# Attention and two MoE stages on one core: a tile's scores in one run of PSUM columns, and what moves with it

## The chip, the core and the metric

One NeuronCore of a Trainium2 chip runs the whole program. The metric is the device time of one execution in microseconds (us): median 1417.6 over three runs, 1417.41 to 1417.85. Five engines work side by side and meet through semaphores: TensorE (PE in the profile: matrix products and transposes, results in PSUM), VectorE (DVE), ScalarE (ACT), GpSimd (POOL) and SyncE (SP, which issues most DMAs). PSUM has eight banks of 512 float32 columns in each of 128 partitions.

## The reference

```python
# attention: B=8, H=8, S=576, D=64; keys and values averaged over 8 neighbours: 72 of each
k_p = k.reshape(B, H, 72, 8, D).mean(axis=3); v_p = ...            # the same
scores = scale * q @ k_p.T;  scores -= max(scores)
attn = exp(scores) / (sum(exp(scores)) + 1e-9);  x = attn @ v_p    # -> 4608 x 512
# moe1: each token goes to its best of 8 experts (512 -> 1024 -> 512)
e = argmax(x @ w_gate + modality_bias[modality_id])
x = gate * (relu(x @ w1[e]) @ w2[e])
# moe2, dense: 512 -> 2048 -> 512
h = x @ w_in;  out = (h * clip(h + 3, 0, 6) / 6) @ w_out
```

## The kernel before

**Attention (0 to about 199 us).** 36 tiles of 128 query rows; one tile holds all eight heads and its 8 x 72 = 576 scores. The fifth tile of a batch holds the last 64 rows of two batches. The loop over tiles is software-pipelined and written out in order: iteration i transposes the exponentials e of tile i (`stage_t`, five transposes and ScalarE's copy eT), takes the exponentials of tile i+2 (`stage_e`, two on ScalarE), scales the second half of the output of tile i-1 (`stage_x`, four on ScalarE), transposes q of tile i+4 (`stage_q`, ScalarE's copy qT), makes the scores of tile i+3 (`stage_s`: eight matmuls, then on VectorE the maximum, L287, and the subtraction, L290 or L293, each once for four heads), and multiplies tile i with the values (`stage_a`: twelve matmuls ups, two halves; on VectorE the sums rs, a reciprocal and the scaling of the first half). Since each engine works in the order in which its instructions were issued, this order is the schedule.

Each batch also needs its keys and values: `pool_kv` averages them (VectorE, L175), `prep` transposes four heads at a time (kvps) and copies them into the block-diagonal key matrix bd (one half by VectorE, L213, one by ScalarE, L214) and vT (L218); `prep2` multiplies the values with the gate weights (pw, L228, L230), which VectorE puts into vb. `sched1` and `sched2` say at which tile. `put_p` makes bp, the form of bd for the mixed tiles. After every group of tiles (`GROUPS`) the routing of its tokens is worked out: `route` and `route_b` give a list `fill` of small operations, of which `run_fill` issues one at fixed places of the stages, mostly on VectorE; `route_b` first issues six short matmuls rps (L416), a running count of tokens per expert.

PSUM in the attention: three banks ps_s, taken in turn by scores (one bank for four heads), kvps, pw and rps; two for the transposes of e; two for ups; one, ps_q, for the transposes of q.

**moe1 (to about 650 us).** Units of 400 tokens of one expert: unit 0, then units in a hardware loop, then two `fs` units and a last one. A unit walks over eight blocks f of the hidden layer: twelve matmuls ph, ScalarE's relu hi and VectorE's rest lo (values are split in two parts for precision), and twelve matmuls y of the block before, over four output banks. In the last block the next unit's tokens are transposed (pt, L856): chunks 0 and 1 ahead of y of block 6, chunks 2 and 3 ahead of y of block 7. Each chunk becomes xhi (ScalarE) and xlo (VectorE) before its bank of two is free again; tkr is a small copy after chunk 0. At the unit's end four copies bring y to SBUF (L1024). Beside this the units prepare moe2's weights: w_in by `conv` (18 operations a call, `ops`), blocks of w_out by `wo_conv`, those in `EARLY` within the `fs` units, those in `REST` in moe2.

**moe2 (to the end).** 6 x 8 `quad`s of products with split weights. Conversions of w_out (`cops`, nine operations a block, on VectorE and ScalarE) are dealt out over the quads of the first of six token groups: two at each of seven places.

Of the kernel before, what the change touches and what calls it, by code (L numbers as in the profile page):

```python
# [19 lines left out]
P = 128  # L20
# [21 lines left out]
EARLY = (0, 8, 1, 9, 2, 10)  # L42
REST = (3, 11, 4, 12, 5, 13, 6, 14, 7, 15)
# [30 lines left out]
def attention(tc, g, moe, ins, xr_d):  # L74
# [122 lines left out]
    def put_v(b, ps):  # L197
        vTs[b] = p2.tile([P, HK], F32, name="vT", tag="vT")
        nc.scalar.copy(vTs[b][64:128].rearrange("p (z x) -> p z x", z=2), ps.rearrange("p (z x) -> p z x", z=2)[64:128, :, 0:288])

    def prep_v(b):
        ps = kv_ps()
        kv_t(b, 2 * D, ps)
        put_v(b, ps)

    def prep(b, z, which="kv"):
        ps = ps_s.tile([P, 512], F32, name="kvps", tag="s")
# [14 lines left out]
    def prep2(b):  # L222
        vT = vTs.pop(b)
        x = kvq.pop(b)
        pw = ps_s.tile([P, 512], F32, name="pw", tag="s")
# [22 lines left out]
    def stage_q(i):  # L248
        b, t = tiles[i]
        ps = ps_q.tile([P, 512], F32, name="qps", tag="q")  # L250
# [16 lines left out]
    def stage_s(i):  # L267
# [11 lines left out]
        mx = p3.tile([P, 2, 4, 1], F32, name="mx", tag="mx")  # L279
        for x in range(2):  # L280
            ps = ps_s.tile([P, 512], F32, name="sps", tag="s")
            for a in range(2 * x, 2 * x + 2):
                for b, p0, p1 in halves(i):
                    rhs = bd[b % 3][:, 4 * hh + a] if t < 4 else bp[b % 3][:, a]
                    nc.tensor.matmul(ps[p0:p1, 144 * (a % 2):144 * (a % 2) + 144], o[:, a, p0:p1], rhs, start=True, stop=True)
            s4 = ps[:, 0:288].rearrange("p (h k) -> p h k", k=SP)
            nc.vector.tensor_reduce(mx[:, x], s4, AX.X, ALU.max)  # L287
            run_fill()
            if t < 4:
                nc.vector.tensor_tensor(d.rearrange("p t (h k) -> p h t k", k=SP)[:, 2 * x:2 * x + 2], s4.rearrange("p (h t) k -> p h t k", t=2),  # L290
                                        mx[:, x].rearrange("p (h t) o -> p h t o", t=2).to_broadcast([P, 2, 2, SP]), op=ALU.subtract)
            else:
                nc.vector.tensor_tensor(d[:, x].rearrange("p (h k) -> p h k", k=SP), s4, mx[:, x].to_broadcast([P, 4, SP]), op=ALU.subtract)  # L293
            run_fill()
# [28 lines left out]
    def stage_a(i):  # L323
        o = ETt.pop(i)
        if i == NTI - 2:
            u = [ps_s.tile([P, 512], F32, name="ups", tag="s")[:, 0:4 * UX].rearrange("p (j x) -> p j x", x=UX) for z in range(2)]
        else:
            u = [ps_u.tile([P, 4, UX], F32, name="ups", tag=f"u{z}") for z in range(2)]
# [80 lines left out]
    def route_b(new=lambda: ps_s.tile([P, 512], F32, name="rps", tag="s")):  # L409
# [77 lines left out]
    sched1, sched2 = {}, {}  # L487
# [10 lines left out]
    wps = ps_q.tile([P, 512], F32, name="wps", tag="q")  # L498
    for _ in range(WU):
        nc.tensor.matmul(wps, zb[:, 0:P], zb[:, 0:512], start=True, stop=True)  # L500
# [24 lines left out]
    kv_t(0, D, ps, (1,))  # L525
    put_k(0, ps, (1,))
# [7 lines left out]
    prep_v(0)  # L534
# [6 lines left out]
    at2(0, lambda: pool_kv(1, 1, v_, rs=(4,)))  # L541
# [7 lines left out]
    at2(3, lambda: prep2(1))  # L549
    for b in range(2, B):  # L550
# [9 lines left out]
        at2(first[b] - o + 2, lambda b=b: (put_p(b), prep2(b)))  # L560
# [17 lines left out]
    for i in range(NTI - 3):  # L578
# [24 lines left out]
        for fn_ in sched1.get(i, ()):  # L603
            fn_()
# [18 lines left out]
    xq = lambda: ps_q.tile([P, 512], F32, name="xps", tag="q")  # L623
    xs = lambda: ps_s.tile([P, 512], F32, name="xps", tag="s")
# [174 lines left out]
def moe1(tc, g, xr_d, tok_d, y_d, s_d, w1, w2, w_in):  # L799
# [83 lines left out]
    def store_y(col):  # L883
# [440 lines left out]
```

## Time and profile before

| | |
|---|---|
| median of three runs | 1417.6 us (1417.41 to 1417.85) |
| the profiled execution | 1416.87 us, its span 1415.1 us |
| mean granted TensorE clock | 0.992 |
| TensorE busy | 1368.4 us, 97% of the span, 7594 instructions |
| VectorE busy | 947.2 us, 67%, 1929 |
| ScalarE busy | 627.6 us, 44%, 1276 |
| GpSimd busy | 159.3 us, 11%, 191 |

A busy share is a mean over three stages with different limits, so stretches are read apart. A timeline row gives start, length, engine, line of the kernel, operation, what it writes and reads with its shape, and in brackets how long the engine was idle before it and whose end released it. A row may stand for several equal instructions (xN). Matmul ends are modelled: a row's length may overlap the next row. A row on a stretch gives its two ends and its length, then busy us and instructions of TensorE, of its weight loads, of VectorE, ScalarE and GpSimd, the granted TensorE clock as a share of full speed, the DMA share and GB/s. A row on a group gives line, engine, operation, its shape and count, busy us and the mean ns of one, and the idle time before them by releaser.

### The profile page before, as it was taken

To read this page: it belongs to the slowest core of one execution; us is meant where nothing else is said; L and a number is where in the kernel's file an instruction comes from. 1 tells how busy PE (TensorE), PEld (TensorE's weight loads), DVE (VectorE), ACT (ScalarE), POOL (GpSimd) and SP (SyncE) were. 2 spreads that over 40 slices of the span, in tenths; PEclk is the share of its full clock that TensorE was granted. 3 is DMA by queue.
4 is the path that set the end of the run, shared out by engine and by line. 5 is a ranking of instruction groups with operands and counts; after the bars stand their busy time and mean duration, and the time that the engine had idled before them with its cause. 6 is when DMAs were issued, how large, how long until landed. Compare 5 with 4: busy or idle time off the path is not lost.

```text
span 1415.1 us, 24118 instructions
## 1 busy us (share of the span) xinstructions
PE 1368.4 (97%) x7594; PEld 1263.5 (89%) x7594; DVE 947.2 (67%) x1929; ACT 627.6 (44%) x1276; POOL 159.3 (11%) x191
## 2 busy tenths in 40 slices
PE   7998989999999999999999999999999999999997
PEld 5888878999999999998888889888988888888886
DVE  6999785788888887876777445645644564465443
ACT  3576664555555554553444333423432343243322
POOL 3132331111111111100000100100010010001001
PEclk8899999999999999999999999999999999999999
DMA  9996356777777776675653544554354455345441
GB/s 254 314 273 203 108 167 197 245 245 246 246 244 243 243 241 199 188 223 169 202 163 114 184 142 120 159 162 119 120 181 140 120 150 173 116 119 164 115 116 67
DMA packets 229781, 254.40 MB, mean 180 GB/s; under 512 B 19256, under 2 KB 191836, under 8 KB 229692
## 3 DMA queue, kind: packets, MB, share of 16 engines
q1 hardware_dynamic: 223932, 233.16, 54.7%
q0 software_dynamic: 5760, 20.10, 4.0%
q8 instruction: 50, 0.82, 0.3%
q14 instruction: 39, 0.32, 0.1%
HBM read 206.74 MB, written 46.47 MB: 179 GB/s over the span
## 4 chain that ended last, share of the span: by engine, by line
issue 56%; PE 3%; POOL 2%; DVE 1%; ACT 0%; POOLq 0%; DVEq 0%; ACTq 0%
POOL out_dram L1074 2%; PE ph L922 2%; PE y L935 1%; DVE wl L772 0%; DVE wo L795 0%; DVE lo L927 0%; PE pt L856 0%; POOLq L1319 0%; ACT wh L771 0%; ACT dex L780 0%; DVE dex L794 0%; DVE dm L785 0%; DVE da L783 0%; ACT hi L926 0%; POOLq L1074 0%
## 5 line engine op out<-in xcount | busy, mean ns | idle before, releaser
L1095 PE MATMUL hps<-yc,sq 128*128 128x384 f32 x2004 | 405.2, 337 | 3.0 <-ACT s L1136 1.2
L1095 PEld LDWEIGHTS hps<-yc,sq 128*128 128x128 f32 x2004 | 358.2, 188 | 37.1 <-ACT s L1136 5.4
L1085 PE MATMUL ops<-wo,gh 128*128 128x512 f32 x1152 | 358.4, 392 | 0.0
L1085 PEld LDWEIGHTS ops<-wo,gh 128*128 128x128 f32 x1152 | 211.4, 188 | 23.1
L1085 PE MATMUL ops<-wo,gl 128*128 128x512 f32 x576 | 228.7, 397 | 0.0
L1107 ACT ACTIVATE r<-c,three 128x384 f32<-128x384 f32 x144 | 88.9, 617 | 207.8 <-DVE c L1117 205.8
L772 DVE TENSOR_TENSOR wl<-ws,wh 128x512 fp32r<-128x512 f32 x192 | 137.8, 751 | 33.4 <-ACT wh L771 29.3
L1111 ACT CAST gh<-r 128x384 fp32r<-128x384 f32 x192 | 98.6, 514 | 129.5 <-DVE r L1108 128.1
L771 ACT CAST wh<-ws 128x512 fp32r<-128x512 f32 x192 | 114.4, 619 | 76.0 <-DMA ws<-in_moe_w_dram 58.2
L922 PE MATMUL ph<-xhi,wh 128*128 128x400 f32 x384 | 132.3, 345 | 3.5 <-issue 1.3
L935 PE MATMUL y<-hi,wh 128*128 128x400 f32 x384 | 134.0, 349 | 0.1
L935 PE MATMUL y<-lo,wh 128*128 128x400 f32 x384 | 132.5, 345 | 1.3 <-DVE lo L927 1.3
L922 PE MATMUL ph<-xlo,wh 128*128 128x400 f32 x384 | 132.7, 346 | 0.2 <-DVE xlo L772 0.2
L922 PE MATMUL ph<-xhi,wl 128*128 128x400 f32 x384 | 132.7, 345 | 0.0
L935 PE MATMUL y<-hi,wl 128*128 128x400 f32 x384 | 131.4, 342 | 0.0
L1085 PEld LDWEIGHTS ops<-wo,gl 128*128 128x128 f32 x576 | 107.9, 187 | 23.1
L1112 DVE TENSOR_TENSOR gl<-r,gh 128x384 fp32r<-128x384 f32 x192 | 106.4, 554 | 27.5 <-ACT gh L1111 23.2
L1074 POOL DMA_INDIRECT out_dram<-osb,tki x36 | 35.3, 981 | 775.3 <-ACT osb L1072 743.5
L1108 DVE SCALAR_TENSOR_TENSOR r<-r,c 128x384 f32<-128x384 f32 x144 | 80.3, 558 | 55.3 <-ACT r L1107 53.4
L848 POOL TENSOR_TENSOR cxg<-cxg 100x512 f32<-100x512 f32 x48 | 57.7, 1205 | 343.8 <-PE ph L922 214.8
L1108 DVE SCALAR_TENSOR_TENSOR r<-r,hps 128x384 f32<-128x384 f32 x48 | 26.6, 553 | 97.6 <-ACT r L1107 96.1
L1107 ACT ACTIVATE r<-hps,three 128x384 f32<-128x384 f32 x48 | 27.9, 581 | 131.7 <-PE hps L1095 129.2
(220 smaller groups left out, 1908.1 us busy)
## 6 DMA issues: line engine op xcount, KB each, us to landing
sq<-sd SPq DMA_DIRECT2D x336, 256.0 KB
ws<-in_moe_w_dram SPq DMA_DIRECT2D x192, 256.0 KB, 3.8
sd<-wq SPq DMA_DIRECT2D x16, 896.0 KB, 4.1
cxg<-xr SPq DMA_DIRECT2D x44, 225.8 KB
yd<-yo SPq DMA_DIRECT2D x12, 800.0 KB, 5.7
yr<-yd SPq DMA_DIRECT2D x12, 768.0 KB
cs<-in_moe_w_in_dram SPq DMA_DIRECT2D x34, 256.0 KB, 3.8
kv<-in_k_dram SPq DMA_DIRECT2D x16, 512.0 KB
```

The lines of the kernel that those rows point to most:

```text
L771: nc.scalar.copy(hi, src)
L772: nc.vector.tensor_tensor(lo, src, hi.bitcast(F32), op=ALU.subtract)
L848: nc.gpsimd.tensor_tensor(s.xg[:, t, 0:DM].rearrange("p (h x) -> p h x", x=D), v, s.xg[:, t, GC:GC + 1].unsqueeze(2).to_broadcast([T4, H, ...
L922: nc.tensor.matmul(ph, a[j][:, 0, k * P:(k + 1) * P], b[k], start=(n == 0), stop=(n == 11))
L935: nc.tensor.matmul(yps[d], a[j][:, 1, d * P:(d + 1) * P], b, start=(f == 0 and n == 0), stop=(f == 7 and n == 2))
L1074: i_ = nc.gpsimd.indirect_dma_start(out=out, out_offset=bass.IndirectOffsetOnAxis(ap=tki[:, c:c + 1], axis=0), in_=o, in_offset=None).ins
L1085: nc.tensor.matmul(pso[t_], gt[a][:, t * P:(t + 1) * P], wo[f][:, b], start=(q == 0 and fh == th and n == 0), stop=(q == NQ - 1 and fh != ...
L1095: nc.tensor.matmul(ps, w[:, kk, a * P:(a + 1) * P], y[:, b, kk], start=(start and n == 0), stop=(n == 5), skip_group_check=True)
L1107: a_.activation(r, c, AF.Relu, bias=g.three)
L1108: v.scalar_tensor_tensor(r, r, 6.0, c, op0=ALU.min, op1=ALU.mult)
L1111: a_.copy(gh, r)
L1112: late.append(lambda: v.tensor_tensor(gl, r, gh.bitcast(F32), op=ALU.subtract))
```

## The change

Scores of a tile lie in columns 224 to 799 of a tile of two banks: four heads end at the bank's border, 512, and four begin there. There is one maximum and one subtraction per tile; the four fills of the stage are kept, two behind each. ps_q is gone: ps_s now has two slots of two banks, and `psb` gives them to q transposes, scores, kvps, pw, rps and later users. The key copy of VectorE in `prep` is ScalarE's, so that ScalarE makes three copies in a tile with k/v preparation. In the loop, `prep` and `prep2` stand behind `stage_a`, and so does `route_b` for tiles below 25.

In moe1 the copies of y stand at the start of the next unit, and the y matmuls of block 7 are split around the third and fourth transposes. The operations of `conv` are dealt out (3, 5, 5, 4, 5, 4, 0, 0) over the blocks instead of five from block 1 on. Two blocks of w_out go from moe2 into the last unit, and moe2's first quad converts none.

```diff
-EARLY = (0, 8, 1, 9, 2, 10)
+EARLY = (0, 8, 1, 9, 2, 10, 3, 11)
...
-    ps_s = pool("ps_s", 3, es_p, space=PSUM)
+    ps_s = pool("ps_s", 2, es_p, space=PSUM)
...
-    ps_q = pool("ps_q", 1, es_p, space=PSUM)
+    psb = lambda name: ps_s.tile([P, 1024], F32, name=name, tag="s")
...
     def prep(b, z, which="kv"):
-        ps = ps_s.tile([P, 512], F32, name="kvps", tag="s")
+        ps = psb("kvps")
...
-            nc.vector.tensor_copy(bd[b % 3][64:128, 4 * z:4 * z + 4, SP:2 * SP], k8)
+            nc.scalar.copy(bd[b % 3][64:128, 4 * z:4 * z + 4, SP:2 * SP], k8)
...
     def stage_q(i):
-        ps = ps_q.tile([P, 512], F32, name="qps", tag="q")
+        ps = psb("qps")[:, 0:512]
...
+        ps = ps_s.tile([P, 1024], F32, name="sps", tag="s")
+        for a in range(4):
...
+                nc.tensor.matmul(ps[p0:p1, 224 + 144 * a:368 + 144 * a], o[:, a, p0:p1], rhs, start=True, stop=True)
+        s8 = ps[:, 224:800].rearrange("p (h k) -> p h k", k=SP)
+        nc.vector.tensor_reduce(mx, s8, AX.X, ALU.max)
+        run_fill()
+        run_fill()
...
-        for fn_ in sched1.get(i, ()):
-            fn_()
...
-        fill.extend(route_b())
+        if i >= 25:
+            fill.extend(route_b())
         stage_a(i)
+        for fn_ in sched1.get(i, []) + sched3.get(i, []):
+            fn_()
+        if i < 25:
+            fill.extend(route_b())
...
     def unit(i, first=False, last=False, tail=None, quad=None, fs=None):
+        if not first:
+            y_out()
...
+        y_mm(7, (0, 1))
         if not last:
-            for c in range(2, 4):
-                transp(c, ps())
-        y_mm(7)
-        for d in range(4):
-            (nc.scalar.copy if d % 2 else nc.vector.tensor_copy)(s.yo[:, d], yps[d])
+            transp(2, ps())
+        y_mm(7, (2,))
+        if not last:
+            transp(3, ps())
+        y_mm(7, (3,))
+        if last:
+            y_out()
...
-            if j == 0:
-                for i in range(7):
-                    for _ in range(2):
+            if j == 0 and q:
+                for i in range(6):
+                    for _ in range(3 if i == 0 else 2):
```

TensorE around the first rps, before: in tile 7, behind the scores and pw, ahead of the output matmuls (five rps matmuls on `ones` follow the one on `tri`).

```order
L311 MATMUL tps<-idn,e 128x128 x5
L256 MATMUL qps<-idn,q 128x128 x4
L285 MATMUL sps<-bd_135,qT 128x144 x4
L228 MATMUL pw<-wg,vT 128x64 x4
L230 MATMUL pw<-wg,vT 32x64 x2
L416 LDWEIGHTS tri
L416 MATMUL rps<-ohs,tri 128x48
...
L332 MATMUL ups<-vb_131,eT 128x146 x6
```

TensorE at the same rps in the changed kernel, from the end of tile 6.

```order
L309 MATMUL ups<-vb_128,eT 64x146
L185 MATMUL kvps<-idn,kvq 128x128 x3
L393 LDWEIGHTS tri
L393 MATMUL rps<-ohs,tri 128x48
...
L287 MATMUL tps<-idn,e 128x128 x5
L231 MATMUL qps<-idn,q 128x128 x4
L259 MATMUL sps<-bd_132,qT 128x144 x4
L309 MATMUL ups<-vb_128,eT 128x146 x6
L203 MATMUL pw<-wg,vT 128x64 x4
```

rps and the k/v transposes now stand behind the output matmuls of tile 6, and pw behind those of tile 7; q and the scores of the next tiles come while rps holds a slot.

VectorE at the first rps, before (tile 7): rps has two readers, base and run, both fills of the stage behind the scores.

```order
L287 TENSOR_REDUCE mx<-sps 128x4
L290 TENSOR_TENSOR d<-sps,mx 128x2x2x72
L239 TENSOR_TENSOR vb_132<-pw,mk 128x8x8
L241 TENSOR_TENSOR vb_132<-pw,mk 64x4x8
L175 TENSOR_TENSOR kv<-kv 128x5x128
L175 TENSOR_TENSOR kvq<-kv 128x5x64
L340 TENSOR_SCALAR rs<-ups 128x4
L434 TENSOR_TENSOR base<-run,rps 128x40
L340 TENSOR_SCALAR rs<-ups 128x4
L435 TENSOR_TENSOR run<-run,rps 128x8
```

VectorE at the same rps in the changed kernel.

```order
L319 RECIPROCAL rs<-rs 128x8
L379 TENSOR_SCALAR gs<-gs 128x5
L322 TENSOR_TENSOR xg<-ups,rs 128x288
L364 RECIPROCAL xg<-gs 128x5
L261 TENSOR_REDUCE mx<-sps 128x8
L411 TENSOR_TENSOR base<-run,rps 128x40
L412 TENSOR_TENSOR run<-run,rps 128x8
L265 TENSOR_TENSOR d<-sps,mx 128x4x2x72
```

base and run now stand between the next maximum and its subtraction; run is the last reader of the rps tile.

TensorE at the end of unit 0, before: all eight transposes between y of block 6 and y of block 7.

```order
L935 MATMUL y_2770<-hi,wh_2521 128x400
L935 MATMUL y_2770<-hi,wl_2525 128x400
L935 MATMUL y_2770<-lo,wh_2521 128x400
L856 MATMUL pt<-idn,cxg 128x100 x8
L935 MATMUL y_2767<-hi,wh_2522 128x400
L935 MATMUL y_2767<-hi,wl_2526 128x400
```

TensorE at the same end in the changed kernel.

```order
L921 MATMUL y_2658<-lo,wh_2417 128x400
L836 MATMUL pt<-idn,cxg 128x100 x4
L921 MATMUL y_2659<-hi,wh_2417 128x400
L921 MATMUL y_2659<-hi,wl_2421 128x400
L921 MATMUL y_2659<-lo,wh_2417 128x400
L836 MATMUL pt<-idn,cxg 128x100 x4
L921 MATMUL y_2660<-hi,wh_2417 128x400
```

Chunks 2 and 3 now have matmuls of block 7 ahead of each; the bank of the last output comes after all transposes.

## Rows read from the trace of the kernel before

**Rows 1.** Busy time in three stretches of the attention:

```profile
37.70:71.00 33.30, 29.79 (x239) 27.74 (x237) 29.68 (x84) 19.72 (x57) 6.61 (x8) 0.90 1.08 311
71.00:150.40 79.40, 71.72 (x626) 66.69 (x624) 73.81 (x226) 56.20 (x163) 27.85 (x27) 1.00 0.71 223
150.40:187.00 36.60, 32.28 (x269) 29.92 (x268) 28.95 (x110) 24.91 (x73) 11.48 (x12) 1.00 0.38 112
```

**Rows 2.** Timeline of one plain tile:

```profile
178.44 0.71 PE L311 MATMUL tps<-idn,e 128*128 128x128 f32 x5
179.24 0.69 ACT L313 COPY eT<-tps 128x640 f32<-128x640 f32 x1 [1.23 <-PE tps L311]
179.42 1.15 PE L285 MATMUL sps<-bd,qT 128*128 128x144 f32 x8
180.51 0.95 ACT L353 ACTIVATE xg<-ups,rs 128x72 f32<-128x72 f32 x4
181.51 1.01 PE L332 MATMUL ups<-vb,eT 128*128 128x146 f32 x6 [0.19 <-ACT xg L353]
182.36 0.71 PE L311 MATMUL tps<-idn,e 128*128 128x128 f32 x5
```

**Rows 3.** Timeline of ScalarE in a tile with k/v preparation:

```profile
98.75 0.39 ACT L214 COPY bd<-kvps 64x288 f32<-64x288 f32 x1 [0.87 <-DVE bd L213]
```

**Rows 4.** Timeline of TensorE around rps in two tiles:

```profile
67.78 0.22 PE L416 MATMUL rps<-ohs,tri 128*128 128x48 bf16 x1 [1.71 <-DVE d L290]
67.99 3.17 PE L332 MATMUL ups<-vb,eT 128*128 128x146 f32 x12
...
92.64 0.20 PE L416 MATMUL rps<-ohs,tri 128*128 128x48 bf16 x1 [1.27 <-DVE d L293]
92.80 1.74 PE L332 MATMUL ups<-vb,eT 128*128 128x146 f32 x12
```

**Rows 5.** Groups by line on VectorE, 71 to 150.4 us:

```profile
L287 DVE TENSOR_REDUCE mx<-sps 128x4 f32<-128x288 f32 x34 | 15.2, 446 | 1.1 <-PE sps L285 1.1
L290 DVE TENSOR_TENSOR d<-sps,mx 128x288 f32<-128x288 f32 x30 | 13.7, 457 | 1.2
L175 DVE TENSOR_TENSOR kv<-kv 128x1280 f32<-128x1280 f32 x8 | 11.9, 1482 | 0.1
L175 DVE TENSOR_TENSOR kv<-kv 128x640 f32<-128x640 f32 x8 | 6.6, 820 | 0.1
L213 DVE COPY bd<-kvps 64x288 f32<-64x288 f32 x8 | 3.6, 450 | 0.3
```

**Rows 6.** The same for ScalarE, line L214:

```profile
L214 ACT COPY bd<-kvps 64x288 f32<-64x288 f32 x8 | 3.1, 393 | 8.5 <-DVE bd L213 8.0 <-issue 0.6
```

**Rows 7.** Busy time and granted clock in two stretches of 5 us:

```profile
65.00:70.00 5.00, 3.29 (x26) 3.06 (x26) 4.90 (x18) 2.61 (x9) 0.00 (x0) 0.75 1.08 344
137.00:142.00 5.00, 3.32 (x32) 3.08 (x31) 4.83 (x15) 3.69 (x11) 0.00 (x0) 1.00 0.00 0
```

**Rows 8.** Timeline of ScalarE at the start:

```profile
31.74 0.76 ACT L214 COPY bd<-kvps 64x288 f32<-64x288 f32 x2 [4.33 <-DVE bd L213]
```

**Rows 9.** Timeline of TensorE at the end of unit 0:

```profile
234.68 0.34 PE L935 MATMUL y<-hi,wl 128*128 128x400 f32 x1
234.86 0.35 PE L935 MATMUL y<-lo,wh 128*128 128x400 f32 x1
236.17 0.56 PE L856 MATMUL pt<-idn,cxg 100*128 100x100 f32 x4 [0.96 <-ACT tkr L861]
237.16 0.56 PE L856 MATMUL pt<-idn,cxg 100*128 100x100 f32 x4 [0.43 <-DVE xlo L772]
237.50 0.43 PE L935 MATMUL y<-hi,wh 128*128 128x400 f32 x1
```

**Rows 10.** Groups by line on TensorE in moe1, line L856:

```profile
L856 PE MATMUL pt<-idn,cxg 100*128 100x100 f32 x176 | 21.1, 252 | 4.3 <-ACT tkr L861 2.7 <-DVE xlo L772 1.6
```

**Rows 11.** Groups by line on TensorE, 652 to 682 us, line L1095:

```profile
L1095 PE MATMUL hps<-yc,sq 128*128 128x384 f32 x71 | 14.8, 343 | 2.4 <-ACT s L1136 1.2 <-DVE ww L1117 0.7 <-DVE c L1117 0.5
```

More of the change, by code (lines that the diff above doesn't have):

```diff
@@ L224, in prep2 @@
         x = kvq.pop(b)
[L225 removed]
+        pw = psb("pw")
         v3 = vT.rearrange("p (z x) -> p z x", z=2)
@@ L278, in stage_s @@
         d = p3.tile([P, 2, 288], F32, name="d", tag="d")
[L279 to L294, printed above, removed]
+        mx = p3.tile([P, H, 1], F32, name="mx", tag="mx")
+        ps = ps_s.tile([P, 1024], F32, name="sps", tag="s")
+        for a in range(4):
+            for b, p0, p1 in halves(i):
+                rhs = bd[b % 3][:, 4 * hh + a] if t < 4 else bp[b % 3][:, a]
+                nc.tensor.matmul(ps[p0:p1, 224 + 144 * a:368 + 144 * a], o[:, a, p0:p1], rhs, start=True, stop=True)
[3 more added lines that the diff above has]
+        run_fill()
+        if t < 4:
+            nc.vector.tensor_tensor(d.rearrange("p t (h k) -> p h t k", k=SP), s8.rearrange("p (h t) k -> p h t k", t=2),
+                                    mx.rearrange("p (h t) o -> p h t o", t=2).to_broadcast([P, 4, 2, SP]), op=ALU.subtract)
+        else:
+            nc.vector.tensor_tensor(d.rearrange("p x (h k) -> p (x h) k", k=SP), s8, mx.to_broadcast([P, H, SP]), op=ALU.subtract)
+        run_fill()
+        run_fill()
         if t < 4:
@@ L325, in stage_a @@
         if i == NTI - 2:
-            u = [ps_s.tile([P, 512], F32, name="ups", tag="s")[:, 0:4 * UX].rearrange("p (j x) -> p j x", x=UX) for z in range(2)]
+            t = psb("ups")
+            u = [t[:, 512 * z:512 * z + 4 * UX].rearrange("p (j x) -> p j x", x=UX) for z in range(2)]
         else:
@@ L407, in route, with route_b @@
         return crit[:5] + [probs] + crit[5:] + rest
-    def route_b(new=lambda: ps_s.tile([P, 512], F32, name="rps", tag="s")):
+    def route_b(new=lambda: psb("rps")):
         ops = []
@@ L497, in attention @@
     v_, p_ = nc.vector, nc.gpsimd
-    wps = ps_q.tile([P, 512], F32, name="wps", tag="q")
+    wps = psb("wps")
     for _ in range(WU):
-        nc.tensor.matmul(wps, zb[:, 0:P], zb[:, 0:512], start=True, stop=True)
+        nc.tensor.matmul(wps[:, 0:512], zb[:, 0:P], zb[:, 0:512], start=True, stop=True)
     load_kv(0, 0, (0, 2))
@@ L533, in attention @@
     stage_e(0)
-    prep_v(0)
+    for z in range(2):
+        prep(0, z, "v")
     stage_e(1)
@@ L827, in open_ps @@
         s.pst = pool("pst", 2, es_p, space=PSUM)
+        s.y = [s.psy.tile([P, NW], F32, name=f"y{d}") for d in range(4)]
     def open3():
@@ L881, in first_x, with y_out, store_y @@
         return i_
-    def store_y(col):
-        return nc.sync.dma_start(y_d.rearrange("(d p) n -> p d n", p=P)[:, :, bass.ds(col, NW)], s.yo)
+    def y_out():
+        for d in range(4):
+            (nc.scalar.copy if d % 2 else nc.vector.tensor_copy)(s.yo[:, d], s.y[d])
+    def store_y(col, a=0, b=4):
+        nc.sync.dma_start(y_d.rearrange("(d p) n -> p d n", p=P)[:, a:b, bass.ds(col, NW)], s.yo[:, a:b])
     def conv_load(c, h, half):
@@ L912, in unit @@
         e = s.e0 if first else reg(0, i, E - 1)
-        yps = [s.psy.tile([P, NW], F32, name=f"y{d}", tag=f"y{d}") for d in range(4)]
+        yps = s.y
         hh = {}
+        if not first:
+            y_out()
         def h_mm(f):
@@ L928, in h_mm, with y_mm @@
             hh[f] = (hi, lo)
-        def y_mm(f):
+        def y_mm(f, ds=range(4)):
             j = f % 4
-            hi, lo = hh.pop(f)
-            for d in range(4):
+            hi, lo = hh[f]
+            for d in ds:
                 for n, (a, b) in enumerate(((s.wh, hi), (s.wl, hi), (s.wh, lo))):
@@ L959, in unit @@
                 store_tok(NT if first else reg(5, i + 1, NT))
-            if f == 3 and not first:
+            if fs is not None and f in (3, 5):
+                store_y(col, f - 3, f - 1)
+            elif fs is None and not first and f == (3 if last else 2):
                 store_y(col)
```

67 lines of the change are left out of this document (24 added, 43 removed).

## The prediction

> **What bounds the kernel now.** I read the busy time by stretch first, then one plain tile of the attention, then the tiles that carry more, and last the ends of the MoE units. From tile 8 to tile 25 the attention takes 79.4 us: VectorE is busy for 73.8 of them, TensorE for 71.7, ScalarE for 56.2. From 150 to 187 us it is VectorE 29.0, TensorE 32.3, ScalarE 24.9 of 36.6 [rows 1]. So by shares alone VectorE looks like the bound of the first stretch (93%), and not of the second (79%).
>
> The order of the waits tells something else. In a plain tile (178.44 to 182.36, 3.92 us) TensorE starts the e transposes at T; ScalarE's copy eT starts 0.80 later; eT, two exps and the four scalings of the last tile fill ScalarE until it releases the second half of the output matmuls, 2.27 after eT began; 0.85 after that the next transposes start [rows 2]. 0.80 + 2.27 + 0.85 = 3.92: the whole tile is one loop over TensorE and ScalarE, and neither the max nor the subtraction lies on it. 17 such tiles would take 66.6 us and 79.4 were needed, a mean of 4.67: the 0.75 per tile on top belongs to the tiles with k/v preparation, pw and rps, and there VectorE has a part. In a k/v tile ScalarE waits 0.87 for VectorE's half of the bd copy [rows 3]; in a tile with rps TensorE stands 1.27 or 1.71 us for a subtraction [rows 4]. Behind the attention TensorE is the bound, and what can be won there is its pauses.
>
> **The change part by part.**
>
> *Scores in one tile.* Two maxima of 446 ns and two subtractions of 457 ns go [rows 5]: 1.81 us. What a 128x576 operation costs no row shows. It lies between 457 (no growth) and 914 (twice). Between the two additions of line L175, 1482 ns at 1280 elements and 820 at 640 [rows 5], the slope is 1.034 ns per element and the rest 158 ns; at 288 that gives 456, which is what the two rows have. So I take 754 and 763, together 1.52, and 0.29 us less VectorE per tile, 10.4 us over 36 tiles; bounds 0 and 32. Nothing of it lies on the loop of a plain tile, so its first price there is 0. The single max can start only when all eight heads are there, 1.15 us after the first score matmul; it ends its subtraction no later than now.
>
> [...]
>
> *bd copy to ScalarE.* Some 14 copies of 0.45 leave VectorE (6.3 us) and become ScalarE's, 0.39 each [rows 5, 6]. VectorE's 0.87 wait goes, but the place moves too: kvps now stands behind the output matmuls. ScalarE's three copies start when these and three transposes (0.6, from five in 0.71) are through, 2.27 + 0.85 + 0.6 = 3.72 after eT, and end 1.2 later, where the next eT can start: a k/v tile becomes 4.94 us, all of it on the loop. Tiles 8, 9, 13, 18 and 21 are such.
>
> *pw behind the output matmuls.* The scores of the next tile need its slot, which VectorE's vb releases; the same walk gives 5.18 per pw tile. Tiles 10, 14, 19, 23.
>
> *Two slots shared by q, scores, k/v, pw and rps.* This is what I fear most. Up to tile 24 the rps matmuls now come at the end of a tile, and their slot is given back only by two fills behind the next max. So in the following tile the q transposes and the scores have one slot for both: the scores wait for that same tile's qT copy, which ScalarE makes behind its scalings. They start 2.83 after eT (2.22 to the end of the scalings, 0.61 for qT) where they start 0.18 after it now [rows 2], and TensorE takes the output matmuls behind them. With the transposes of k/v at its end such a tile (12, 17, 22) becomes 0.80 + 2.83 + 1.15 scores + 1.74 output [rows 4] + 0.6 = 7.1 us. The pauses of 1.27 and 1.71 [rows 4] go.
>
> Tiles 8 to 24 by this walk: 5 x 4.94 + 3 x 7.1 + 4 x 5.18 + 2 x 4.2 (plain with rps, 11 and 16) + 3 x 3.92 = 86.9, against 79.4: +7.5. Bounds: 0 when the waits for VectorE that go are worth as much, +12 when slips add up. From tile 25 rps stands ahead of the output matmuls as now: +0.5. Tiles 2 to 7 are 89% VectorE [rows 1] and lose 6 x 0.29 and four copies of 0.45, 3.5 us of its time; their own walk gives -0.2 with one late tile (7) among them. I take -1. At the start ScalarE's 4.33 us behind VectorE's bd [rows 8] goes, but the two k halves of batch 1 now come after more work: -1.8 (bounds -3 and 0). Last tiles +0.2. Attention together: +7.5 + 0.5 - 1 - 1.8 + 0.2 = +5.4.
>
> *moe1, unit ends.* The last y matmul of block 6 starts at 234.86 and the next could at 235.04, since they follow each other by 0.18. The eight transposes stall twice, 0.96 and 0.43, and y goes on at 237.50 [rows 9]; without a stall they cost two times 0.34, so 237.50 - 235.04 - 0.68 = 1.78 is lost where 1.39 shows as idle. All unit ends of the stage show 4.3 us of idle [rows 10]; times 1.78/1.39 that is 5.5. With six y matmuls (1.1 us) ahead of the third transposes and three ahead of the fourth, tkr, which lets go at 236.17, is in time, and xlo (237.16) about 0.1 late. Gain 5.3; bounds 1.5 and 7. The four y copies move into the next unit, beside the twelve first ph matmuls, and cost nothing unless they hold up xhi and xlo of the last x chunk, needed some 1.6 us later. The conversions of w_out that come into the last unit add VectorE work there: +0.2.
>
> *moe2, start.* In the first two quads TensorE waits for s, ww and c, which ScalarE and VectorE make behind conversions: 2.4 in sum [rows 11]. The first quad converts none now. Gain 2.4; bounds 0 and 3. MoE together: -5.3 + 0.2 - 2.4 = -7.5.
>
> Sum against the profiled execution: 1416.87 + 5.4 - 7.5 = 1414.8; it lay 0.7 under the median of 1417.6, so in terms of that I say 1415.5.
>
> **Rivals.**
>
> *A, VectorE sets the pace of the attention.* For it: 93% busy from tile 8 to 24 [rows 1], and each wait in the k/v and rps tiles ends on VectorE [rows 3, 4]. Against it: the plain tile closes without it. It loses 10.4 + 6.3 = 16.7 us; if half of it comes back as time, and the late scores are hidden by the three tiles that stage s runs ahead, the attention gains about 6 (start included) and the time is 1417.6 - 6 - 7.5 = 1404. All of it back would be 1393.
>
> *B, the shared slots cost more than the MoE gives (the other side).* In the tiles after rps TensorE stands some 2.5 us. Where it stood 1.71 (65 to 70 us), its granted clock fell to a mean of 0.75, and twelve output matmuls took 3.17 instead of 1.74 [rows 4, 7]. Against it: 137 to 142 has as little TensorE work and kept 1.00 [rows 7]. If all four such tiles (7, 12, 17, 22) fall, each costs about 2.5 more: +10, attention +16, 1417.6 + 16 - 7.5 = 1426. It decides once the attention loses over 7.5 + 2.8.
>
> *C, the MoE gain does not come.* The unit ends may wait for the same xlo in two places instead of one, and y copies in front of xhi may delay it. The MoE then gives 1.5 instead of 7.5: 1422. Against it: 1.1 us of matmuls now lies where 0.96 was waited for [rows 9].
>
> [...]
>
> **How the numbers follow.** A measurement here can tell 0.2% (2.8 us) from no change: the same means 1414.8 to 1420.4. My forecast has 0.38, its own range 1410 to 1420.5: 0.10 faster, 0.24 same, 0.04 slower. A has 0.36, nearly all faster (0.35). B has 0.14, slower. C has 0.12: 0.04 same, 0.08 slower. Together, with A's last 0.01, faster 0.45, same 0.29, slower 0.26. The range takes in the lesser half of A and of B and C nearly all: 1401 to 1427.
>
> **What would show it.** In the profile after: one max and one subtraction per tile of 0.75 us each; plain tiles still 3.92; k/v tiles near 4.9 with ScalarE's idle behind VectorE gone; scores that wait for ScalarE's qT in tiles 7, 12, 17 and 22, and these tiles at about 7 us (at 1.00 clock for the forecast, below for B); 79.4 turned into about 87; unit ends without the two stalls; no wait over 0.5 in the first moe2 quad. If the stretch of tiles 8 to 24 falls below 79, my loop is wrong and VectorE was the bound; if the unit ends keep their pauses, C is right.

## The result, and the profile after

The changed kernel takes 1431.3 us (median of six executions, 1429.58 to 1439.21), the one before 1417.5 (six, 1416.55 to 1418.27): ratio 1.0105, 95% interval 1.0082 to 1.0127. It is slower, outside the range of the prediction. The profiled execution is the slowest of the six, 1439.21; of its distance to before some 8 us are its own.

The profile's page after: span, TensorE's row, the granted clock in 40 slices.

```profile
span 1437.4 us, 24012 instructions
...
PE 1383.8 (96%) x7594; PEld 1276.8 (89%) x7594; DVE 932.4 (65%) x1841; ACT 630.9 (44%) x1293; POOL 154.0 (11%) x191
...
PEclk8979999999999999999999999999999999999999
```

The third slice (72 to 108 us) is at 7, where before it was at 9; the mean over the span is 0.983 instead of 0.992. The stretches that answer to [rows 1], tiles 2 to 7, 8 to 24 and 25 to 32 (columns as there):

```profile
37.71:76.77 39.06, 32.92 (x239) 29.51 (x237) 30.38 (x76) 20.93 (x61) 7.67 (x9) 0.85 0.85 237
76.77:179.02 102.25, 83.78 (x626) 75.40 (x624) 66.98 (x179) 59.32 (x171) 25.49 (x27) 0.91 0.53 175
179.02:217.61 38.59, 33.96 (x269) 31.60 (x268) 26.78 (x92) 25.55 (x75) 10.50 (x11) 0.96 0.33 96
```

Tiles 8 to 24 take 102.25 us instead of 79.40, tiles 2 to 7 39.06 instead of 33.33. VectorE's busy time in tiles 8 to 24 fell from 73.81 to 66.98, its share from 93% to 66%: it is lighter by 6.8 us, and the stretch is 22.9 longer. Its two operations per tile (compare [rows 5]):

```profile
L261 DVE TENSOR_REDUCE mx<-sps 128x8 f32<-128x576 f32 x17 | 12.9, 757 | 32.3 <-PE sps L259 25.6 <-issue 3.7 <-PE ups L309 3.0
L265 DVE TENSOR_TENSOR d<-sps,mx 128x576 f32<-128x576 f32 x15 | 11.4, 757 | 0.9
```

757 ns each, as worked out (754 and 763; one of half the length took 446 and 457 [rows 5]). Now TensorE in the tile behind an rps, tile 12 (compare [rows 4]; the name tps is the e transposes, qps q's, sps the scores):

```profile
99.87 0.20 PE L393 MATMUL rps<-ohs,tri 128*128 128x48 bf16 x1 [0.49 <-DVE ohs L374]
99.91 0.27 PE L393 MATMUL rps<-ohs,ones 128*128 128x40 bf16 x5
100.04 0.74 PE L287 MATMUL tps<-idn,e 128*128 128x128 f32 x5
100.62 0.60 PE L231 MATMUL qps<-idn,q 128*128 128x128 f32 x4
103.62 2.19 PE L259 MATMUL sps<-bp,qT 128*64 128x144 f32 x16 [2.40 <-ACT qT L233]
105.73 3.29 PE L309 MATMUL ups<-vb,eT 128*128 128x146 f32 x12
108.82 0.85 PE L185 MATMUL kvps<-idn,kvq 128*128 128x128 f32 x3
109.46 0.74 PE L287 MATMUL tps<-idn,e 128*128 128x128 f32 x4
```

The rps matmuls stand at the end of tile 11 and wait 0.49. Then the scores stand 2.40 us for ScalarE's qT: the mechanism of the prediction, at its place and length. But the scores then take 2.19 and the twelve output matmuls 3.29 instead of 1.66 in the tile before, and the tile takes 9.42 us, not 7.1. The granted clock of this execution says why (stretches of 5 us, columns as above, the clock ahead of the last two):

```profile
95.00:100.00 5.00, 3.82 (x34) 3.40 (x33) 3.56 (x15) 2.83 (x9) 0.00 (x0) 1.00 0.02 4
100.00:105.00 5.00, 2.60 (x27) 2.35 (x27) 2.72 (x10) 2.69 (x8) 1.62 (x2) 0.79 0.47 162
105.00:110.00 5.00, 5.00 (x27) 4.60 (x24) 4.01 (x12) 0.30 (x1) 0.00 (x0) 0.53 0.29 100
```

From 1.00 it goes to 0.79 in the stretch with the pause and 0.53 in the next, where TensorE is busy for all 5.00 us; in stretches of 1 us it is 1.00 up to 102 us, 0.50 in each from 103 to 109 and 1.00 again from 110. Tiles 7, 12, 17 and 22 take 11.52, 9.42, 8.12 and 8.37 us. That is one execution, the slowest; `attn_only` below shows the same tile with the same wait and no fall of the clock.

A k/v tile and the pw tile after it (all engines):

```profile
114.37 0.71 PE L287 MATMUL tps<-idn,e 128*128 128x128 f32 x5
...
115.40 0.39 ACT L193 COPY vT<-kvps 64x288 f32<-64x288 f32 x1
115.82 0.69 ACT L289 COPY eT<-tps 128x640 f32<-128x640 f32 x1
...
118.09 1.01 PE L309 MATMUL ups<-vb,eT 128*128 128x146 f32 x6 [0.24 <-ACT xg L330]
119.03 1.10 PE L203 MATMUL pw<-wg,vT 64*128 64x64 f32 x8
...
120.30 0.76 PE L287 MATMUL tps<-idn,e 128*128 128x128 f32 x5
```

vT, the last of ScalarE's three copies, makes eT start 1.45 after the e transposes, not 0.80; then comes the loop of 2.27 to the second output half, and pw behind it adds its 1.27 before the next transposes: 5.93 us, against 5.18 forecast. Plain tiles are 3.92 still.

At the end of a unit of moe1 (compare [rows 9]) both transposes now follow y without a pause:

```profile
267.78 0.34 PE L921 MATMUL y<-lo,wh 128*128 128x400 f32 x1
267.96 0.51 PE L836 MATMUL pt<-idn,cxg 100*128 100x100 f32 x4
268.24 0.43 PE L921 MATMUL y<-hi,wh 128*128 128x400 f32 x1
...
268.69 0.35 PE L921 MATMUL y<-lo,wh 128*128 128x400 f32 x1
268.88 0.55 PE L836 MATMUL pt<-idn,cxg 100*128 100x100 f32 x4
269.21 0.43 PE L921 MATMUL y<-hi,wh 128*128 128x400 f32 x1
```

By the starts of stages in the two traces, the attention (to the first ph) is 33.5 us longer, moe1 6.7 shorter (444.6 from 451.3) and moe2 4.4 shorter (762.7 from 767.1): +22.3, the difference of the spans.

### The profile page after: what moved, and what is told of

Its sections match the earlier page's. It is cut to its first block, busy times and chain, and to the rows that moved or that the text cites. A ratio compares the mean times of both kernels' runs of the same rounds, so it can differ in the third digit from the quotient of the medians.

```text
span 1437.4 us, 24012 instructions
## 1 busy us (share of the span) xinstructions
PE 1383.8 (96%) x7594; PEld 1276.8 (89%) x7594; DVE 932.4 (65%) x1841; ACT 630.9 (44%) x1293; POOL 154.0 (11%) x191
## 4 chain that ended last, share of the span: by engine, by line
issue 54%; POOL 2%; PE 2%; DMA 1%; DVE 1%; ACT 0%; POOLq 0%; SPq 0%; ACTq 0%; DVEq 0%
POOL out_dram L1069 2%; PE ph L908 1%; DMA ws<-in_moe_w_dram 1%; PE y L921 1%; DVE wl L751 0%; DVE lo L913 0%; ACT wh L750 0%; DVE dex L773 0%; DVE wo L774 0%; POOLq L1314 0%; ACT dex L759 0%; DVE dm L760 0%; PE pt L836 0%; ACT hi L912 0%; POOLq L1069 0%
## 5 line engine op out<-in xcount | busy, mean ns | idle before, releaser
L1106 ACT CAST gh<-r 128x384 fp32r<-128x384 f32 x192 | 98.7, 514 | 130.3 <-DVE r L1103 128.9
L751 DVE TENSOR_TENSOR wl<-ws,wh 128x512 fp32r<-128x512 f32 x192 | 131.8, 724 | 18.2 <-ACT wh L750 17.9
L1103 DVE SCALAR_TENSOR_TENSOR r<-r,c 128x384 f32<-128x384 f32 x144 | 80.4, 558 | 54.7 <-ACT r L1102 52.7
L828 POOL TENSOR_TENSOR cxg<-cxg 100x512 f32<-100x512 f32 x48 | 54.4, 1136 | 341.0 <-PE ph L908 175.8
```

The lines of the kernel that those rows point to most:

```text
L751: nc.vector.tensor_tensor(lo, src, hi.bitcast(F32), op=ALU.subtract)
L828: nc.gpsimd.tensor_tensor(s.xg[:, t, 0:DM].rearrange("p (h x) -> p h x", x=D), v, s.xg[:, t, GC:GC + 1].unsqueeze(2).to_broadcast([T4, H, ...
L1103: v.scalar_tensor_tensor(r, r, 6.0, c, op0=ALU.min, op1=ALU.mult)
L1106: a_.copy(gh, r)
```

## The experiments

Fifteen kernels. A ratio is to the kernel before on the same chip; on one chip that took 1410.3 us, so ratios are compared and not medians. "The changed kernel" is 1.0105.

**Which half** (`moe_only`, `attn_only`). The attention function of one kernel with the rest of the other, both ways (in outline, not the code's own lines).

```diff
-def attention(...) of the one kernel, whole
+def attention(...) of the other, whole
```

> The attention of before with the MoE parts of the change (the y copies, the split transposes, the conversions). In the profile of the changed kernel moe1 begins 30.8 us later than before, and moe2 begins 26.7 and the span ends 22.3 later, so the MoE gains 8.5. If the MoE parts are independent of the attention: 1417.5 - 8.5 = 1409. Rival: part of that gain was only slack that a late attention leaves (weights already loaded): 1413 to 1417.

> The attention of the change with the MoE of before. If both halves add up: about 1431 + 8.5 = 1440. If they don't: nearer to 1431.

Measured: MoE alone 1405.4 us, 0.9926 (0.9909 to 0.9943); attention alone 1444.5, 1.0210 (1.0189 to 1.0232). 0.9926 x 1.0210 = 1.0135, so the halves nearly add up. The MoE's gain is real and larger than forecast (about 11 instead of 7.5); the expectation's 8.5 rests on a start of moe1 30.8 us later, where the first ph row gives 33.5. The attention costs about 28 to 30, not 5.4.

The trace of `attn_only` is a second execution of the changed attention. Tile 12 in it, and the stretches of 5 us around it:

```profile
98.89 1.20 PE L259 MATMUL sps<-bp,qT 128*64 128x144 f32 x16 [2.39 <-ACT qT L233]
100.02 1.76 PE L309 MATMUL ups<-vb,eT 128*128 128x146 f32 x12
```

```profile
90.00:95.00 5.00, 3.96 (x33) 3.49 (x29) 3.56 (x14) 2.82 (x9) 0.00 (x0) 1.00 0.53 172
95.00:100.00 5.00, 2.46 (x31) 2.04 (x31) 3.00 (x11) 2.69 (x8) 1.61 (x2) 1.00 0.51 142
100.00:105.00 5.00, 4.58 (x36) 4.13 (x35) 4.66 (x13) 2.81 (x8) 0.39 (x1) 1.00 0.47 147
```

The wait for qT is the same, 2.39 us, and the clock stays at 1.00. Tiles 12 and 17 take 6.63 and 6.48 us there (tile 22, where the clock falls, 8.53), tiles 8 to 24 94.52 instead of 102.25. So the fall of the clock comes and goes from execution to execution, and at full clock in these tiles the attention is still some 28 us slower.

**rps ahead of the output matmuls everywhere** (`rps_early`).

```diff
-        if i >= 25:
-            fill.extend(route_b())
+        fill.extend(route_b())
         stage_a(i)
...
-        if i < 25:
-            fill.extend(route_b())
```

> The changed kernel with rps ahead of the output matmuls in every tile, so that its slot is given back within the same tile. Theory 1 (after rps q and the scores have one slot for both, the scores wait 2.15 to 2.40 for qT, and the granted clock falls to half behind that): the waits of the scores for qT in tiles 7, 12, 17, 22 go and with them most of the slow clock, 1431 becomes 1415 to 1421. Rival (with two slots any place of rps costs a pause of that size: rps now waits some 2 us for ohs on VectorE ahead of the output matmuls, and the clock falls all the same): 1427 to 1432.

Measured: 1426.6, 1.0069 (1.0045 to 1.0093): on the 1417.5 of before that is 1427, the near edge of the rival's range, and the interval overlaps with that of the changed kernel. The scores no longer wait for qT behind rps, but rps now waits for its slot until a qT copy is done: 7.8 us in five waits, up to 1.9. Tiles 12, 17 and 22 take 5.87, 5.59 and 6.21 us, and the clock is 1.00 from 95 us on; but k/v and pw tiles stay at 4.87 and 5.92.

**Keeping TensorE at work in the pause** (`warm`).

```diff
+        if i in (7, 12, 17, 22):
+            dm = ps_t.tile([P, 1024], F32, name="dmy", tag="t")
+            for _ in range(10):
+                nc.tensor.matmul(dm[:, 0:512], zb[:, 0:P], zb[:, 0:512], start=True, stop=True)
         stage_s(i + 3)
```

> The changed kernel with ten matmuls of zeros (128x512, bfloat16) put into a free tile between the q transposes and the scores of tiles 7, 12, 17 and 22, where TensorE stands. The waits stay. If the fall of the granted clock behind the pause is what made these tiles and the next so long, they run at full clock and the time falls by 8 to 14 us (1417 to 1423). If the clock does not follow this pause, the time stays at 1431 or rises by up to 2.

Measured: 1425.8, 1.0073 (1.0047 to 1.0098). Tile 12 of its trace, TensorE:

```profile
96.69 2.32 PE L580 MATMUL dmy<-zb 128*128 128x512 bf16 x9 [0.40 <-ACT eT L289]
98.94 1.20 PE L259 MATMUL sps<-bp,qT 128*64 128x144 f32 x16
100.07 1.76 PE L309 MATMUL ups<-vb,eT 128*128 128x146 f32 x12
```

The filler stands where the pause was, the scores start 3.83 us after the e transposes instead of 3.58, and the output matmuls behind take 1.76 instead of 3.29; the clock is 1.00 in every 25 us from 70 on. The tile takes 6.88 us (17 and 22: 6.54 and 6.97), which is the 7.1 of the prediction at full clock. So the medians put the fall of the clock at about 0.3% (4.5 us), which is less than I expected; the intervals overlap, and nothing at all is not ruled out. With it gone, tiles 8 to 24 still take 93.3 us.

**The old order with the new slots** (`order_of_before`). k/v, pw and rps ahead of `stage_a` again.

```diff
-        for fn_ in sched2.get(i, ()):
+        for fn_ in sched1.get(i, []) + sched2.get(i, []) + sched3.get(i, []):
             fn_()
-        if i >= 25:
-            fill.extend(route_b())
+        fill.extend(route_b())
         stage_a(i)
-        for fn_ in sched1.get(i, []) + sched3.get(i, []):
-            fn_()
-        if i < 25:
-            fill.extend(route_b())
```

> The changed kernel with k/v preparation, pw and rps ahead of the output matmuls, as before; the two slots, the single max and the ScalarE copies stay. Theory 1 (what costs is that q, scores and the others share two slots): kvps, now behind the scores and ahead of the output matmuls, must wait for that tile's qT copy, 2.2 us after the scores, in each of the 14 k/v tiles; they become 6 to 7 us and the time rises to 1440 to 1470. Rival (what costs is the new order alone): k/v tiles fall from 4.9 to 4.2 and pw tiles from 5.9 to 4.9, and the time falls to 1405 to 1415.

Measured: 1429.1, 1.0074 (1.0049 to 1.0099). Neither number came true, but the waits did (TensorE, 60 to 200 us: total, times, longest):

```profile
PE kvps L185 <- ACT qT L233: 16.2, 11, 1.9
PE pw L203 <- ACT qT L233: 6.3, 4, 2.1
```

With two slots, kvps and pw behind the scores must wait for that tile's qT: 22.5 us in 15 waits, 1.5 each and not the 2.2 forecast. Pauses in these tiles take the place of ScalarE's late copies. Neither of the two orders is free with two slots: the changed one avoids these waits and pays in others, and the two times don't differ by more than their intervals.

**The key copy back on VectorE** (`bd_dve`).

```diff
-            nc.scalar.copy(bd[b % 3][64:128, 4 * z:4 * z + 4, SP:2 * SP], k8)
+            nc.vector.tensor_copy(bd[b % 3][64:128, 4 * z:4 * z + 4, SP:2 * SP], k8)
```

> The changed kernel with the second half of the key copy back on VectorE, which is busy 70% now. If ScalarE's three copies (0.41 each) lie on the loop of a k/v tile, one less gives 14 x 0.4 = 5.7 us: 1425 to 1427 against 1431. Rival (ScalarE then waits for VectorE as it did before, 0.87 in a tile, because it stays in order behind the averaging of k/v): 1431 to 1436.

Measured: 1453.8, 1.0267 (1.0250 to 1.0284). I was wrong by its sign and size. ScalarE in tile 13 of its trace, and TensorE's largest wait from 60 to 200 us:

```profile
114.64 0.39 ACT L189 COPY bd<-kvps 64x288 f32<-64x288 f32 x1 [6.29 <-DVE bd L188]
```

```profile
PE sps L259 <- ACT vT L193: 16.7, 8, 3.1
```

1.6% is lost against the changed kernel, well outside the intervals. VectorE's copy comes behind averaging, rs and the scaling in VectorE's order; until it is done, ScalarE's vT and the slot of kvps are held, and the scores of the next tile stand up to 3.1 us. The copy on ScalarE is what makes two slots bearable. Neither of my theories had the slot's release in it.

**Two maxima and two subtractions on the same columns** (`two_max`).

```diff
-        nc.vector.tensor_reduce(mx, s8, AX.X, ALU.max)
+        for x in range(2):
+            s4, m4 = s8[:, 4 * x:4 * x + 4], mx[:, 4 * x:4 * x + 4]
+            nc.vector.tensor_reduce(m4, s4, AX.X, ALU.max)
```

(and the subtraction likewise, inside the loop, with one fill behind each)

> The changed kernel with two maxima and two subtractions of four heads each on the same columns: 0.29 us more VectorE per tile, 10 in all. If VectorE is off the loop of the tiles: 1430 to 1434. If VectorE sets the pace in part: 1436 to 1442.

Measured: 1435.7, 1.0144 (1.0122 to 1.0166), against 1.0105. The medians put the merge at some 0.4% within this kernel, where 10 us of VectorE's time would be 0.7%; the intervals just overlap, so anything from nothing to 0.8% fits, and its trace has tiles 8 to 24 at 98.7 us, not above 102.25. This run does not settle how much VectorE sets the pace.

**rps in free columns of ups**, of its first bank, its place in the order kept (`rps_ups`).

```diff
+            ul[:] = [u[0][:, 320:512]]
...
-            fill.extend(route_b())
+            fill.extend(route_b(lambda: ul[0]))
```

> The changed kernel with rps, at the same place of the order for tiles below 25, in free columns of the output bank ups, so that it takes no slot from q and the scores. Theory 1: the scores of tiles 7, 12, 17 and 22 no longer wait 2.15 to 2.40 for qT; the output matmuls of these tiles wait about 1.1 for base and run instead; the clock falls less: 1419 to 1425 against 1431. Rival (the place of rps in the order costs, not its slot): 1429 to 1433.

Measured: 1433.5, 1.0126 (1.0102 to 1.0150): no gain. The pause moved (TensorE, around tile 12):

```profile
96.53 0.20 PE L397 MATMUL ups<-ohs,tri 128*128 128x48 bf16 x1 [3.32 <-DVE xg L326]
101.55 1.73 PE L313 MATMUL ups<-vb,eT 128*128 128x146 f32 x12 [1.25 <-DVE run L416]
```

rps, now in an output bank, waits 3.32 for VectorE's scaling of tile 11 out of that bank, and the next output matmuls wait 1.25 for run. The scores' waits for qT are gone. Behind the pause of 3.32 the clock falls too (0.66 from 95 to 100 us), but over the whole program its mean is 0.994, as high as in the kernel before, and the time is that of the changed kernel. The pauses cost their own length first, the clock comes on top.

**base and run at once** (`run_now`).

```diff
-            ops += route_c(j, ps, *rt.pop(j))
+            c_ = route_c(j, ps, *rt.pop(j))
+            c_[0]()
+            c_[1]()
+            ops += c_[2:]
```

> The changed kernel with the two readers of rps, base and run, issued right behind the rps matmuls instead of as fills behind the next maximum; place and slot of rps stay. Theory 1 (the scores behind rps wait for qT because rps holds the second slot): the waits of 2.15 to 2.40 in tiles 7, 12, 17 and 22 go, and the slow clock behind them: 1431 becomes 1416 to 1422. Rival (VectorE is so far behind there that the slot comes free no earlier): 1428 to 1432.

Measured: 1415.8 on a chip where before takes 1410.3, 1.0039 (1.0025 to 1.0053): 0.7% better than the changed kernel, about 9 us. The slot held by two fills was worth that much, with what the clock had of it. In tile 12 the scores still wait, for run now, but the clock is 1.00 (95 to 120 us):

```profile
98.26 1.20 PE L259 MATMUL sps<-bp,qT 128*64 128x144 f32 x16 [1.94 <-DVE run L415]
99.39 1.76 PE L309 MATMUL ups<-vb,eT 128*128 128x146 f32 x12
```

Tiles 12, 17 and 22 take 6.18, 4.28 and 5.50. Tile 4 (8.24), k/v tiles (4.87) and pw tiles (5.92) are as in the changed kernel, and most of what is left lies there. Tiles 8 to 24 take 86.8 us, 7.4 more than before.

**Is it sharing, or only two slots?** (`share4`). The MoE of the change and the attention of before, scores in two halves; q in one pool with the others, but of four slots of one bank.

```diff
-    ps_s = pool("ps_s", 3, es_p, space=PSUM)
-    ps_q = pool("ps_q", 1, es_p, space=PSUM)
+    ps_s = pool("ps_s", 4, es_p, space=PSUM)
...
-        ps = ps_q.tile([P, 512], F32, name="qps", tag="q")
+        ps = ps_s.tile([P, 512], F32, name="qps", tag="s")
```

> The MoE of the change and the attention of before, but q transposes share one pool of four one-bank slots with scores, k/v, pw and rps; scores stay in two tiles with two maxima. If sharing as such makes q, scores and the rest wait for each other's copies: 1412 to 1430. If the loss comes from the size, two banks for each user and so only two slots: 1403 to 1409 (1405.4 with q apart).

Measured: 1398.4 on the chip with before at 1410.3, 0.9925 (0.9901 to 0.9950); with q apart it was 0.9926. Sharing alone costs nothing that these runs can show. What is left is the size: a tile of two banks per user leaves two slots for a chain that has up to four users in a tile. This run also has the order and the two maxima of before; the order, put back by itself, gained nothing clear (`order_of_before`), and two maxima none (`two_max`). The new order with four slots was not run.

**The single maximum without shared slots** (`own_banks`). Against `moe_only`, with the single maximum and subtraction of the change:

```diff
-    ps_s = pool("ps_s", 3, es_p, space=PSUM)
+    ps_s = pool("ps_s", 1, es_p, space=PSUM)
+    ps_m = pool("ps_m", 1, es_p, space=PSUM)
...
-    def route_b(new=lambda: ps_s.tile([P, 512], F32, name="rps", tag="s")):
+    def route_b(new=lambda: tl[0][:, 512:1024]):
```

ps_s is one score tile of two banks, ps_m one bank for k/v and pw; q keeps its bank, and rps goes into the e-transpose tile. Then also with ScalarE's key copies (`own_banks_bd`), then also with base and run at once (`own_run_now`); their lines are those of the other experiments, and the last also gives the transposes of unit 0's tokens, at the end of the attention, two places instead of one.

> The MoE of the change and the attention of before in its order, with the single maximum and subtraction over 576 columns, but PSUM dealt out anew: one score tile of two banks, q in a bank of its own, k/v and pw in another, rps in the free columns of the e-transpose tile. Theory 1 (the loss came from the shared slots, not from the merged operations): no wait of scores, kvps or pw for qT, the granted clock stays at 1.00 from 75 us on, and VectorE is 0.29 per tile lighter: 1398 to 1405 (1405.4 without the merge). Rival (the merged operations cost by themselves, as the scores wait for one subtraction over all heads): 1410 or more.

> The last one with the second half of the key copy on ScalarE too. If VectorE still ends the waits in the k/v tiles: 2 to 4 us less than that one. If ScalarE's loop does: the same or up to 3 more.

> The kernel with a bank for each user, ScalarE's key copies and the single maximum (1409), with base and run issued right behind rps, and the transposes of unit 0's tokens at the end in two slots again. Its transposes of e waited 7.5 us for the slot of rps and its last part 4.1 for the one bank. If these are gone and nothing comes in their place: 1398 to 1403. If VectorE, made to wait for rps, passes it on: 1404 to 1410.

Measured: 1427.3, 1.0085 (1.0059 to 1.0110); 1409.1, 0.9956 (0.9941 to 0.9971); 1406.1 on the faster chip, 0.9973 (0.9963 to 0.9982). None beats 0.9926.

`own_banks_bd` has the merged operations, ScalarE's key copies and the loop order of `order_of_before`; apart from the k/v of the first two batches at the start, only the places in PSUM differ. That makes 1.0074 against 0.9956, 1.2% and clear of the intervals, and tiles 8 to 24 take 78.7 us against 97.2. This is the cost of the two shared slots with all else nearly equal. What the kernels with own places lose against `moe_only` does not lie in these tiles (78.7 and 78.5 us in the last two, 80.4 there) but behind them: from tile 33 to the first ph `own_banks_bd` takes 18.3 us where `moe_only` takes 10.5. In `own_run_now`, TensorE from 20 to 210 us:

```profile
PE tps L316 <- DVE run L444: 7.1, 5, 1.6
PE ph L939 <- DVE base L445: 3.7, 1, 3.7
```

Most k/v and pw tiles are at 3.9 and 4.9 us there, but rps needs a place, and this one stops the next e transposes. That base and run wait for rps on VectorE and TensorE then for run is not mended by issuing them early. Between the first two, the key copy makes 1.3% here; in the attention of before (`moe_bd`, the same line in `moe_only`) it makes none:

> The attention of before and the MoE of the change (1405.4), with the second half of the key copy on ScalarE, where the k/v preparation stands ahead of the output matmuls. ScalarE's wait for VectorE (15.9 us in the profile before, 0.87 in a tile) goes, VectorE loses 14 copies. If VectorE sets the pace of the attention of before: 1399 to 1403. If the loop over TensorE and ScalarE does: 1404 to 1409, since the copy is one more on ScalarE.

Measured: 1404.9, 0.9915 (0.9898 to 0.9931), the same as 0.9926 within the intervals.

**The MoE's unit ends without the split** (`moe_nosplit`, against `moe_only`). The copies of y stay in the next unit.

```diff
-        y_mm(7, (0, 1))
         if not last:
-            transp(2, ps())
-        y_mm(7, (2,))
-        if not last:
-            transp(3, ps())
-        y_mm(7, (3,))
+            for c in range(2, 4):
+                transp(c, ps())
+        y_mm(7)
```

> The attention of before and the MoE of the change, but with all of the third and fourth transposes ahead of the y matmuls of block 7. If the split is worth the 5.3 us of the prediction: 1410.7 against 1405.4. If the copies of y at the next unit's start are what lets tkr and xlo be in time: 1405 to 1407.

Measured: 1405.9, 0.9924 (0.9900 to 0.9948): by the times the split is worth nothing that shows. In the traces moe1 takes 449.0 us without and 444.6 with it, and the pauses are back (TensorE, end of unit 0):

```profile
234.60 0.56 PE L857 MATMUL pt<-idn,cxg 100*128 100x100 f32 x4 [1.13 <-ACT tkr L862]
235.59 0.56 PE L857 MATMUL pt<-idn,cxg 100*128 100x100 f32 x4 [0.43 <-DVE xlo L772]
```

The two answers differ by 4 us, about as much as executions of one kernel spread here (1404.1 to 1408.6). Over all unit ends TensorE stands 2.0 us ahead of the transposes, 4.3 in the kernel before and 0.0 with the split: the rest of the change halves it, the split takes the other half. Part of the 449.0 is a lower clock behind the pause (0.66 from 235 to 240 us). The fourteen traces with the split have moe1 at 440.1 to 446.5 us. The trace shows the pause; that the whole time follows it stays open.

## Why the prediction was wrong

**"Attention together: ... = +5.4" is the step that failed.** Alone it costs 2.1%, 28 to 30 us. Its parts in the two traces of the changed attention, against before (us):

| part | forecast | changed kernel | `attn_only` |
|---|---|---|---|
| the start, to tile 2 | -1.8 | 0.0 | -1.2 |
| tiles 2 to 7 | -1 | +5.7 | +5.2 |
| tiles 8 to 24 | +7.5 | +22.9 | +15.1 |
| tiles 25 to 32 | +0.5 | +2.0 | +1.0 |
| tile 33 to the first ph | +0.2 | +2.8 | +3.7 |
| together | +5.4 | +33.5 | +23.8 |

The walk had a slot held for long only behind rps. In the runs vb, which gives back the slot of pw, comes late as well, and the users at the end of the attention wait too; behind the longest waits the clock fell, in one execution more often than in the other (means of 25 us from 70 to 195: 0.75 to 0.93 in all five in the changed kernel; 0.93 in two of five, else 1.00, in `attn_only`).

- **Tiles 8 to 24, 86.9 in the sum,** are 102.25 and 94.52 us. Its terms:
  - *rps tiles, 3 x 7.1.* The wait for qT and its length were right, and 7.1 is not too low at full clock: 6.63 and 6.48 for tiles 12 and 17 in `attn_only`, 6.5 to 7.0 with the filler. In the changed kernel the three take 25.9 together instead of 21.3, for the clock (0.53, 0.80 and 0.72 over the 5 us from 105, 135 and 165), which stood only in rival B with a chance of 0.14; in `attn_only`, where it falls in tile 22 alone of the three, 21.6. In the changed kernel tiles 8 and 9, behind tile 7, also run slow (6.58 and 5.51, at a clock of 0.50 from 75 to 80 us and 0.76 to 85; 4.24 and 4.87 in `attn_only`).
  - *pw tiles, 4 x 5.18.* 5.92 to 5.96 each in both, +3.0. The walk counted from eT to eT (5.28 in tile 14) and left out that the k/v tile's copies delay eT and pw then adds to the end. At full clock a part of it comes back in tile 8, 4.24 against 4.94.
  - *tiles 11 and 16, 2 x 4.2.* 5.26 and 5.34: rps waits for ohs (0.49 in tile 11), and in tile 11 the scores wait 0.69 for vb of the pw tile before.
  - *tile 20, 3.92, and tile 21, 4.94.* 5.54 and 6.19 in the changed kernel: the scores of tile 20 wait 1.79 us for vb of pw tile 19, the output matmuls of tile 21 1.87 for a routing operation of VectorE (L356).
- **"I take -1" for tiles 2 to 7** was +5.7. Tile 7 makes 3.0 of it and tile 4 3.8, where the scores stand for vb. By vb VectorE empties the slot of pw, and it comes to that only behind the averaging of the next batch:

```profile
51.66 2.20 PE L259 MATMUL sps<-bd,qT 128*128 128x144 f32 x8 [2.84 <-DVE vb L216]
53.66 2.38 PE L309 MATMUL ups<-vb,eT 128*128 128x146 f32 x12
```

- **The start, -1.8,** was 0 in the changed kernel (tile 2 begins at 37.71 instead of 37.67) and -1.2 in `attn_only`. **The last tiles, +0.2,** were +2.8 and +3.7: TensorE waits there for VectorE's xlo and xg around the transposes of unit 0's tokens (up to 2.6 us in `attn_only`), which share the two slots.
- **VectorE's price, 0.29 per tile,** was right. That it would come back as time (rival A, 0.36) was wrong: lighter by 6.8 us in tiles 8 to 24, that stretch grew. With a place for each user and ScalarE's key copies the merged operations leave it at 78.5 to 78.7 us, where the attention of before takes 79.4 to 80.4.
- **Rival B** had the sign and the place right, and the clock for the execution traced; but it named the clock as most of the price, and tiles 12 and 17 of `attn_only` kept it while the attention lost all the same. Full clock gives back some 0.3%, not clear of the intervals; an earlier release of the slot of rps 0.7%, the clock's part included. That two slots are the common cause is shown by `order_of_before` against `own_banks_bd` (1.2%), by `run_now` and by `bd_dve`. How the loss divides among the tiles in the new order was not taken apart further.
- **MoE -7.5** was right in sign and 3.5 short: moe1 -6.7 against -5.1, moe2 -4.4 against -2.4. The moe2 waits of [rows 11] are gone; what the other 2 us are was not tried. With the same code moe1 takes 440.1 to 446.5 us from trace to trace, so its -6.7 is known to some 3 us.

The version to keep is the MoE part of the change with the attention of before: 0.9926; with the key copies on ScalarE 0.9915, which is the same within the intervals.

## What to carry to other kernels

When an edit merges two small tiles into a large one, count the slots that are left and walk each slot through one period: who holds it, which engine lets it go, and what stands ahead of that release in this engine's order. Read a wait's price at the clock that was granted behind the pause (0.53 and 1.00 here behind the same one), in more than one execution, and from the same point of one tile to that of the next. An operation made cheaper on an engine off the loop bought some 0.4% here at best, not clear of noise; the two slots that its larger tile left cost 1.2% with all else nearly equal.

## What the runs showed of the hardware

The same pause went both ways. A pause of 2.40 us in TensorE in the changed kernel, after a stretch of 5 us with 3.82 busy, was followed by a mean clock of 0.53 over 5 us, of which TensorE was busy for all 5.00. In `attn_only` a pause of 2.39 us at the same place, after 5 us with 3.96 busy, left 1.00. A pause of 3.32 us in `rps_ups` was followed by 0.66 over 5 us, one of 1.94 in `run_now` by 1.00. So in these four the length of the pause did not tell whether the clock fell, and a price of the clock that is read from one trace holds for that execution.

A maximum and a subtraction over 576 columns that cross a PSUM bank took 757 ns each, against 754 and 763 worked out from shorter operations; the border showed no price.
